# Batch 0's second pair of token tiles by seven products instead of eight, in a kernel whose order is planned

## The chip, the cores and the metric

The kernel runs on one core of a Trainium2 chip. The core has a matrix engine (TensorE, in the profile PE, with its weight loads shown apart as PEld), a vector engine (VectorE, DVE), a scalar engine (ScalarE, ACT), a general engine (GpSimd, POOL) and a queue engine (SyncE, SP). Each takes its instructions strictly in the order in which the program issued them, and waits at an instruction until what it needs is done. The metric is the device time of one execution in microseconds (us), as the median over several runs.

## The reference

Four batches of windowed attention with sink tokens, and a two-layer network with a squared ReLU over all 3072 tokens:

```python
B, H, S, D = 4, 8, 768, 64
keep = (pos[None, :] < 4) | ((rel >= 0) & (rel < 128))
a = softmax(where(keep, q @ k.T / sqrt(D), -1e9))
x = (a @ v).transpose(0, 2, 1, 3).reshape(B * S, H * D)     # 3072 x 512
g = maximum(x @ w_in, 0) ** 2                               # 3072 x 2048
out = g @ w_out                                             # 3072 x 512, float32
```

## The kernel before, in words

**Stages.** Each batch has 768 tokens, six tiles of 128, taken as three pairs of tiles (`s` in the attention, `u` in the second layer). For each batch q and k are transposed, scores are made (`ps`, L749), exponentials taken on ACT (`expm`, L769), masked on DVE (L778, L781) or POOL (L360), multiplied with the values (`po`, L817), normalised on DVE into `xn` (L834), and turned into `xT` (L866 on TensorE in batches 0 and 1, by DMA in 2 and 3). The first layer (`pm`, L895) writes PSUM tiles of 1024 columns; ReLU and square (L906, L908, L915, L917) leave `gT`, in two buffers: columns 0 to 511 (pairs 0 and 1) and 512 to 767 (pair 2). Batch 1's squares into the first buffer wait for the second layer of batch 0's pairs 0 and 1, by a dependency in `square`.

**The second layer has two forms.** `layer2` is the plain one: for each of the two tiles of a pair, 16 matmuls of 512 columns (L936), issued in eight parts of four matmuls, and one copy per tile into `osb` (L334). With `by_part` the two tiles take turns, so that a part needs only a quarter of `w_out` and of the squares. `layer2_fast` is an algebra of the Strassen kind: tiles a and b of the pair and the two halves of the 2048 inner columns make a 2 by 2 block matrix, and the two halves of the output columns another for `w_out`. Seven products of half size, each of eight matmuls of 256 columns (L1047), take the place of eight. It needs four block sums of `gT` on DVE (s1 to s4, L1005, 128 x 1024; s3 is written over tile b's lower half in `gT`, the others into four `sg` buffers), and four differences of blocks of `w_out` (wt1 to wt4, L977), which are made once by `weight_sums`. Its outputs share terms: two quarters are copied out early (`taken`, into `osb` and `u`), and pair sums (L1072), a last quarter (L1088) and the middle two quarters (L1095) are added on DVE before one store on SP (L1120).

In the kernel before, batch 0's pairs 0 and 1 go by `layer2`, its pair 2 and all pairs of batches 1 to 3 by `layer2_fast`. The last line of the call that decides it is `if b == 0 and u < 2` (L1189).

**What sets the order.** No loop of the program is the order of issue. Each step is an `op` with a key (its wanted place), engines with an assumed length on each, and the steps and buffers that it needs. `Plan.run` is a list scheduler: at every turn it takes the ready step with the earliest planned start (plus a lag), the key breaking ties, puts it on the engine where it would end first, and issues its instructions. `LATENCY` is the assumed time from one engine's end to another's start. `PLACES` shifts and stretches the keys of a group of steps and adds a lag; `NUDGES` does so for single steps by their number. Where an engine can be chosen (masks on POOL or DVE, copies on ACT or DVE), the plan chooses it. `warm` adds dummy matmuls (L327) in planned gaps before `WARM_UNTIL`. So the tables decide the order on each engine; on the chip semaphores hold it right whatever the lengths are. The order of the loads in each DMA queue is fixed by `dma_op`, but on POOL the loads stand in one line with its masks and copies.

PSUM has two pools, `att` and `den`, of two tiles each; a pair of the second layer holds one `den` tile from its first matmul to its last output step. There are two `osb` and two `u` buffers.

Of the kernel before, what the change touches and what calls it, by code (L numbers as in the profile page):

```python
# [16 lines left out]
LATENCY = 0.135  # L17
# [5 lines left out]
    ('att', 0, 0): (3.3, 1.08, 0.18), ('att', 0, 1): (3.285, 0.47, 0.38), ('att', 0, 2): (-0.2, 1.41, -0.24),  # L23
    ('att', 1, 0): (-1.415, 2.2, -0.42), ('att', 1, 1): (-0.385, 1.02, -0.22), ('att', 1, 2): (6.08, 1.06, 0.36),
    ('att', 2, 0): (-0.225, 0.25, -0.64), ('att', 2, 1): (-1.615, 1.17, -0.58), ('att', 2, 2): (0, 1.02, -0.06),
    ('att', 3, 0): (-0.075, 1.08, 0.1), ('att', 3, 1): (-0.04, 1.04, 0.04), ('att', 3, 2): (1.235, 0.72, 0.98),
    ('ev', 0, 2): (-0.16, 1.15, 0.78), ('ev', 1, 0): (0.585, 0.56, -0.48), ('ev', 1, 1): (0.47, 1.11, 0.24),
    ('ev', 1, 2): (-0.095, 1.18, 0.08), ('ev', 2, 0): (-0.22, 0.93, 0.28), ('ev', 2, 1): (0.015, 1.02, -0.46),
    ('ev', 2, 2): (1.345, 0.4, 1.32), ('ev', 3, 1): (-0.155, 1, 0.08), ('ev', 3, 2): (-0.055, 1.28, -0.44),
    ('l1', 0, 0): (-0.035, 1.27, 0), ('l1', 0, 1): (0.18, 0.85, 0.08), ('l1', 0, 2): (-0.6, 1.31, -0.4),  # L30
    ('l1', 1, 0): (4.96, 0.3, 0.74), ('l1', 1, 2): (0.265, 1.41, -0.28), ('l1', 2, 0): (-0, 0.59, 0.5),
    ('l1', 2, 2): (0.1, 1.22, -0.12), ('l1', 3, 0): (0.075, 0.91, 0.48), ('l2', 0, 0): (0.055, 0.81, 0.38),
    ('l2', 0, 1): (0.435, 1.16, 0), ('l2', 0, 2): (0.16, 1.12, -0.1), ('l2', 1, 0): (1.05, 0.56, -0.96),
    ('l2', 1, 1): (-0.425, 1.06, -0.1), ('l2', 1, 2): (-0.18, 1.03, 0.2), ('l2', 2, 0): (-0.115, 0.96, 0.58),
    ('l2', 2, 1): (2.185, 1.21, 1.32), ('l2', 2, 2): (2.75, 1, 0.74), ('l2', 3, 0): (-0.765, 0.25, 2.4),
    ('l2', 3, 1): (0.08, 0.81, 0.18), ('l2', 3, 2): (0.23, 1.94, 2.82), ('prep', 0, 0): (2.165, 1.2, -0.5),
    ('prep', 0, 1): (0.115, 1.01, -0.24), ('prep', 1, 0): (0.05, 0.87, 0.08), ('prep', 1, 1): (0.84, 1.23, 0.54),
    ('prep', 2, 0): (-0.005, 0.96, 0.24), ('prep', 3, 0): (-0.045, 1.08, 1.16),
    ('sink', 0, 0): (0.015, 1.11, -0.04), ('sink', 0, 1): (0, 1.12, -0.06), ('sink', 1, 0): (-0.225, 1.01, -0.06),
    ('sink', 3, 0): (-0.565, 0.62, 0.5), ('sum', 0, 2): (-0.14, 0.68, -0.34), ('sum', 1, 0): (-1.615, 0.44, -1.74),  # L40
    ('sum', 1, 1): (0.645, 0.91, -1.4), ('sum', 1, 2): (0.34, 1.45, 0.14), ('sum', 2, 0): (-0.655, 1.85, 0.06),
    ('sum', 2, 1): (-0.24, 1, 0.18), ('sum', 2, 2): (0.405, 1.27, 0.3), ('sum', 3, 0): (0.25, 2.36, 0.94),
    ('sum', 3, 2): (0.185, 1.17, 1.74), ('turn', 0, 0): (-0.56, 2.1, -0.62), ('turn', 0, 1): (0.11, 0.94, -0.14),
    ('turn', 0, 2): (-0.205, 1.01, 0.02), ('turn', 1, 0): (-0.2, 0.94, -0.02),
    ('turn', 1, 1): (-0.345, 1.33, -0.42), ('turn', 1, 2): (1.765, 2.5, -2.14), ('turn', 2, 0): (0, 1.05, 0),
    ('turn', 2, 1): (-0.26, 1.09, -0.3), ('turn', 3, 0): (-0.06, 1.05, -0.44), ('turn', 3, 1): (0.075, 0.56, 0.64),
    ('turn', 3, 2): (0, 1, 0.14), ('val', 0, 0): (0.345, 0.45, -0.28), ('val', 0, 1): (0.69, 0.58, -0.46),
    ('val', 0, 2): (-0.09, 0.78, -0.08), ('val', 1, 0): (-2.595, 0.7, 0.22), ('val', 1, 1): (0.035, 1.14, 0.06),
    ('val', 1, 2): (-0.65, 0.98, 0.64), ('val', 2, 0): (-1.11, 0.59, -1.94), ('val', 2, 1): (0.755, 0.42, -0.3),
    ('val', 2, 2): (-0.425, 1.6, -0.06), ('val', 3, 0): (0.1, 1.17, 0.6), ('val', 3, 1): (0.805, 0.25, 0.74),  # L50
    ('val', 3, 2): (0.105, 0.92, 2.28), ('wt', 0): (-0.205, 0.82, -0.32),
}
NUDGES = {
    4: (-0.022, 0.56), 16: (0, 0.14), 17: (-0.211, -0.38), 18: (0.48, -1.62), 19: (0, 0.4), 20: (0.364, -0.58),
    21: (0.004, 0.16), 22: (0.02, 0), 23: (0.016, 0.18), 24: (-0.06, -0.78), 25: (0.35, 1.84), 26: (-0.106, 0.66),
    27: (0.014, -0.64), 29: (-0.004, 0.86), 30: (0, 0.42), 31: (0.013, 0), 33: (-0.009, 0), 34: (-0.094, 0.5),
    36: (-0.027, 0.16), 37: (0.188, 0.08), 38: (-0.052, 0), 39: (-0.269, -0.82), 40: (-0.004, 0),
    41: (-0.419, 0.34), 42: (0.398, -2.86), 43: (0.134, -0.1), 44: (0.027, 0.14), 45: (0.009, 0), 46: (0.123, 0.66),
    47: (0.073, 0.9), 49: (0, 0.1), 51: (-0.102, -0), 52: (-0.278, -0.06), 53: (-0.001, 0.18), 56: (0.05, 0.1),
    57: (0.049, -0.16), 58: (0.016, -0.78), 60: (-0.008, -0.14), 61: (-0.013, 0), 62: (0, 0.22), 63: (-0.292, -0.2),  # L60
    64: (-0.079, 0.34), 65: (0.028, 0.64), 66: (-0.114, -0.38), 67: (0.099, -0.02), 68: (0.076, -0.28),
    69: (-0.851, 0.68), 71: (0.036, 0.22), 72: (-0.036, -0.24), 73: (0.024, 0.18), 74: (0.02, 0), 75: (-0.063, 0),
    76: (0, -0.04), 78: (0.042, 0.28), 80: (0.009, 0.26), 81: (0.023, 1.36), 82: (-0.02, 0.04), 83: (-0.008, -0.54),
    84: (-0.128, -0.42), 85: (-0.161, -0.36), 86: (0.003, 0), 87: (-0.004, 0.08), 88: (-0.069, 0),
    89: (-0.003, -0.16), 90: (-0.088, 0.02), 91: (0.016, -0.28), 92: (0.109, 0), 93: (0.015, 0.38),
    94: (0.043, -0.24), 95: (0.159, 0.04), 96: (-0.083, 0.04), 97: (-0.05, -0.3), 98: (-0.346, 0.8),
    99: (-0.435, 0.54), 100: (-0.21, -0.52), 101: (0.407, 1.44), 102: (0.013, 0.78), 103: (0.147, -0.08),
    104: (-0.112, -0.16), 105: (-0.121, -0.1), 107: (0.009, 0), 108: (0.214, 0.04), 109: (0.006, 0.08),
    111: (0.033, 0.86), 112: (0.046, 0.56), 113: (0.043, 0.6), 114: (-0.154, 0.42), 115: (-0.084, -0.16),
    116: (-0.145, -0.28), 117: (-0.026, -1.22), 118: (0.126, -0.62), 119: (-0.123, -0.24), 120: (0.115, 0.56),  # L70
    121: (0, -0.14), 122: (-0.121, 0.08), 123: (0, -0.2), 124: (0.034, -0.16), 125: (-0.168, 0.24),
    126: (0.017, -0.44), 127: (0.071, -0.82), 128: (-0.128, 0.1), 129: (-0.006, -0.08), 130: (0, -0.56),
    131: (0.402, 0.04), 132: (-0.056, 0), 133: (0.291, -0.28), 134: (-0.028, 0), 135: (0.064, -1.52),
    136: (-0.069, 0), 137: (-0.061, 0.54), 139: (-0.041, 0.32), 140: (-0.043, 0), 142: (-0.077, -0.12),
    143: (-0.069, 0.14), 144: (0.271, 0.26), 145: (0.008, 0.02), 146: (0.046, -0.52), 147: (0.008, -0.22),
    148: (0.006, 0.26), 149: (-0.028, 0.28), 150: (0.065, 0.06), 151: (0.051, 0.04), 152: (0.164, -0.12),
    153: (-0.401, 0.06), 154: (0.019, 0), 155: (-0.388, -0.64), 156: (-0.112, 1.16), 157: (0.287, 0.94),
    158: (-0.278, 1.3), 159: (-0.002, -0.18), 160: (0.118, 0.3), 162: (0.145, 0.5), 164: (0.158, 0.46),
    165: (0.095, 0), 166: (0.015, 0.02), 167: (0.055, 0), 168: (0.161, -0.48), 169: (-0.217, 0.24),
    171: (0.132, 0.52), 172: (0.011, -0.1), 173: (-0.036, 0.78), 174: (-0.047, -0.16), 175: (0.115, 0),  # L80
    176: (-0.342, 0.18), 177: (0, -0.02), 178: (-0.092, 0.58), 179: (0.041, 0.04), 180: (0.136, 0),
    186: (0.353, 0.28), 187: (-0.073, -0.02), 188: (-0.044, 0.48), 189: (-0.009, 0.06), 190: (0.057, -0.6),
    191: (-0.512, 1.18), 192: (0.405, 0.62), 193: (-0.012, -0.02), 194: (-0.003, 0.04), 195: (0.216, 0.94),
    196: (-0.08, -0.04), 197: (-0.038, 0.14), 198: (0.002, -0.54), 199: (0.12, 0.14), 200: (-0.304, 0),
    201: (-0.106, -0.12), 202: (0.038, 0.08), 203: (-0.001, -0.3), 205: (0.013, -0.44), 206: (-0.01, 0.46),
    207: (-0.003, 0.02), 208: (0.277, 0.98), 209: (0.006, -1.42), 210: (0.099, 0.36), 211: (0.041, 0),
    212: (0.006, 0), 214: (0.108, 0.54), 215: (0.057, 0.38), 216: (0.2, 0.22), 217: (-0.118, -0.12),
    218: (-0.002, 0.26), 219: (0.129, -0.22), 220: (0.008, -0.44), 221: (0.213, 1.02), 222: (0.464, -0.34),
    223: (-0.206, 0.1), 224: (0.064, 0), 225: (0.277, 0.32), 226: (-0.123, 0.62), 227: (0.015, 1.76),
# [170 lines left out]
def kernel(  # L260
# [22 lines left out]
    NKB = DM // 128  # L283
# [33 lines left out]
    op = P.op  # L317
# [566 lines left out]
    def layer1(b, key, fbs, c0, cw, need):  # L884
        P.group = ("l1", b, c0 // 256)
        n = len(fbs)
# [344 lines left out]
```

## Time and profile before

| | us |
|---|---|
| median of 10 runs (215.3 to 216.84) | 216.25 |
| the profiled execution: its own time | 216.69 |
| its span, first to last instruction | 214.9 |
| TensorE busy | 207.2 |
| DVE busy | 147.6 |
| ACT busy | 119.0 |
| POOL busy | 78.2 |
| first layer's matmuls (L895), busy | 87.4 |

A busy matmul is not a matmul's share of the stream: matmuls overlap, and a group's mean (309 ns for L895, 380 ns for L936, 273 ns for L1047) holds the time from its start to its modelled end. The distance from one start to the next is read from pieces of the chain of waits or from the list of instructions in order of time. The mean granted TensorE clock was 0.996.

### The profile page before, as it was taken

To read this page: it belongs to the slowest core of one execution; us is meant where nothing else is said; L and a number is where in the kernel's file an instruction comes from. 1 tells how busy PE (TensorE), PEld (TensorE's weight loads), DVE (VectorE), ACT (ScalarE), POOL (GpSimd) and SP (SyncE) were. 2 spreads that over 40 slices of the span, in tenths; PEclk is the share of its full clock that TensorE was granted. 3 is DMA by queue.
4 is the path that set the end of the run, shared out by engine and by line. 5 is a ranking of instruction groups with operands and counts; after the bars stand their busy time and mean duration, and the time that the engine had idled before them with its cause. 6 is when DMAs were issued, how large, how long until landed. Compare 5 with 4: busy or idle time off the path is not lost.

```text
span 214.9 us, 5183 instructions
## 1 busy us (share of the span) xinstructions
PE 207.2 (96%) x2189; PEld 160.3 (75%) x2189; DVE 147.6 (69%) x282; ACT 119.0 (55%) x149; POOL 78.2 (36%) x112
## 2 busy tenths in 40 slices
PE   7798999999999999999999999999999999999992
PEld 7468996589487645678897955876988955798892
DVE  5687658577958784677778757648886643466852
ACT  3697357455764669977654279769207046671110
POOL 7979474499969830884800000000001100000000
PEclk9999999999999999999999999999999999999998
DMA  5999999999999999999999543000325160000222
GB/s 152 287 172 203 174 199 215 159 128 205 156 137 145 197 217 124 157 122 157 117 220 111 149 104 93 3 0 0 52 98 95 54 149 0 0 3 2 98 101 98
DMA packets 93351, 26.06 MB, mean 121 GB/s; under 512 B 86800, under 2 KB 91280, under 8 KB 93328
## 3 DMA queue, kind: packets, MB, share of 16 engines
q0 software_dynamic: 69248, 12.59, 81.5%
q1 hardware_dynamic: 23896, 13.07, 28.2%
q8 instruction: 17, 0.28, 0.6%
q10 hardware_dynamic: 184, 0.07, 0.1%
q14 instruction: 6, 0.05, 0.1%
HBM read 27.30 MB, written 6.29 MB: 156 GB/s over the span
## 4 chain that ended last, share of the span: by engine, by line
PE 88%; DMA 6%; ACT 2%; DVE 1%; POOL 1%; SPq 0%; issue 0%
PE pm L895 38%; PE py L1047 28%; PE py L936 7%; PE po L817 6%; PE ps L749 5%; DMA w_in_sb<-in_moe_w_in_dram 4%; DMA qr<-in_k_dram 2%; PE pt L642 2%; ACT expm L769 1%; PE ya L1047 1%; PE px L866 1%; DVE xT L336 1%; POOL expm L360 1%; PE pk L708 1%; SPq L491 0%; ACT qs L334 0%
## 5 line engine op out<-in xcount | busy, mean ns | idle before, releaser
L895 PE MATMUL pm<-xT,w_in_sb 128*128 128x256 bf16 (+1 forms) x576 | 87.4, 309 | 0.8 <-DMA w_in_sb<-in_moe_w_in_dram 0.6
L895 PEld LDWEIGHTS <-w_in_sb 128*128 128x128 bf16 x576 | 62.4, 114 | 20.7 <-issue 1.3
L906 ACT ACTIVATE r<-pm 128x1024 bf16<-128x1024 f32 x42 | 43.1, 1025 | 33.0 <-PE pm L895 30.8
L769 ACT ACTIVATE expm<-ps 128x1024 bf16<-128x1024 f32 (+1 forms) x48 | 43.4, 951 | 15.5 <-PE ps L749 15.5
L917 DVE TENSOR_TENSOR gT<-r 128x1024 bf16<-128x1024 bf16 x35 | 24.2, 691 | 22.8 <-ACT r L906 22.6
L1047 PEld LDWEIGHTS <-gT 128*128 128x128 bf16 x336 | 31.1, 98 | 4.5 <-issue 1.2
L360 POOL TENSOR_SCALAR_AFFINE_SELECT expm<-expm 128x512 bf16<-128x512 bf16 x12 | 7.3, 632 | 73.3 <-ACT expm L769 68.7
L1047 PEld LDWEIGHTS <-sg 128*128 128x128 bf16 x240 | 22.9, 98 | 3.0 <-issue 0.5
L781 DVE TENSOR_TENSOR expm<-expm,tri 128x1024 bf16<-128x1024 bf16 x26 | 18.3, 706 | 7.7 <-ACT expm L769 7.5
L1047 PE MATMUL py<-wt,gT 128*128 128x256 bf16 x160 | 20.8, 273 | 0.0
L1047 PE MATMUL py<-wt,sg 128*128 128x256 bf16 x160 | 20.8, 273 | 0.0
L1047 PE MATMUL py<-w_out_sb,gT 128*128 128x256 bf16 x144 | 18.7, 273 | 0.0
L834 DVE TENSOR_TENSOR xn_sb<-po,rc 128x512 bf16<-128x512 f32 (+1 forms) x28 | 17.2, 615 | 1.0
L817 PE MATMUL po<-v,expm 128*128 128x65 bf16 x352 | 17.5, 193 | 0.4 <-DMA v<-in_v_dram 0.2
L817 PEld LDWEIGHTS <-expm 128*128 128x128 bf16 x352 | 16.4, 97 | 1.9 <-issue 0.4
L334 ACT ACTIVATE osb<-py 128x256 f32<-128x256 f32 (+1 forms) x15 | 6.6, 441 | 16.8 <-PE py L1047 11.7
L936 PE MATMUL py<-w_out_sb,gT 128*128 128x512 bf16 x64 | 15.7, 380 | 0.0
L749 PE MATMUL ps<-qkT 64*128 64x128 bf16 (+1 forms) x256 | 14.6, 238 | 0.0
L749 PEld LDWEIGHTS <-qkT 64*128 64x128 bf16 x256 | 8.0, 94 | 8.1 <-issue 7.5
L915 ACT ACTIVATE gT<-r 128x1024 bf16<-128x1024 bf16 x13 | 13.7, 1056 | 0.3
L817 PE MATMUL po<-vs,es 128*128 128x65 bf16 x128 | 13.0, 193 | 0.0
L817 PEld LDWEIGHTS <-es 128*128 128x128 bf16 x128 | 11.7, 97 | 0.3 <-issue 0.3
(78 smaller groups left out, 240.4 us busy)
## 6 DMA issues: line engine op xcount, KB each, us to landing
out_dram<-osb SPq DMA_DIRECT2D x11, 512.0 KB, 3.9
v<-in_v_dram POOLq DMA_DIRECT2D x24, 128.0 KB, 6.1
qn<-in_k_dram POOLq DMA_DIRECT2D x20, 128.0 KB, 8.6
qn<-in_q_dram POOLq DMA_DIRECT2D x20, 128.0 KB, 8.8
w_in_sb<-in_moe_w_in_dram POOLq DMA_DIRECT2D x4, 512.0 KB, 9.6
w_out_sb<-in_moe_w_out_dram POOLq DMA_DIRECT2D x4, 512.0 KB, 10.6
qr<-in_k_dram SPq DMA_DIRECT2D x4, 256.0 KB, 5.4
qr<-in_q_dram SPq DMA_DIRECT2D x4, 256.0 KB, 5.2
```

Source lines behind the costliest of these rows:

```text
L360: nc.gpsimd.affine_select(out=e_tile, in_=e_tile, compare_op=ALU.is_ge, fill=fill, base=i - 1, pattern=[[0, n], [1 if i else -1, 128]], ch ...
L749: nc.tensor.matmul(ps[:, h2, o:o + w], lhsT=qkT_sb[r, m, 1, c, :], rhs=qkT_sb[r, m, 0, qb:qb + w // 128, :], start=(i == 0 and not biased) ...
L769: nc.scalar.activation(out=x[:, :, o:512], in_=bank_t["s", b, s, m][:, :, o:512], func=AF.Exp, scale=scale)
L781: nc.vector.tensor_mul(y, y, tri.rearrange("p (o a) c -> p o (a c)", o=1).to_broadcast([128, 4, 256]))
L817: touch(("po", b, s, m0), e, nc.tensor.matmul(pv[:, i, h2, :], lhsT=lhsT, rhs=rhs, start=(n_ == 0), stop=(n_ == len(mms) - 1)), j)
L834: touch(("po", b, s, m0), e, nc.vector.tensor_tensor(out=xn_sb[:, 2 * s:2 * s + 2, 128 * (m0 + j0):128 * (m0 + j0 + nj)].rearrange("p i (j ...
L895: nc.tensor.matmul(pm[:, i, :], lhsT=w_in_sb[:, fb // 4, kb, fb % 4:512:4], rhs=xT[:, c0 // 256:(c0 + cw) // 256, kb, :], start=(kb == 0), ...
L906: nc.scalar.activation(out=o, in_=h, func=AF.Relu)
L915: nc.scalar.activation(out=g, in_=r, func=AF.Square)
L917: nc.vector.tensor_mul(g, r, r)
L936: touch((b, u), e, nc.tensor.matmul(pm[:, i, :], lhsT=gT_sb[t // 4][:, fb, 128 * (t % 4):128 * (t % 4) + 128], rhs=w_out_sb[:, fb, :], sta ...
L1047: ins = nc.tensor.matmul(y_, lhsT=x[:, i, :], rhs=r_, start=(first or tail and n == 2) and i == 0, stop=i == HB - 1, skip_group_check=not ...
```

## The change

Batch 0's pair 1 goes by `layer2_fast` instead of `layer2`. The planner's constants and all entries of both tables are new, so the order of issue is another one throughout:

```diff
-LATENCY = 0.135
+LATENCY = 0.261
 PLACES = {
-    ('att', 0, 0): (3.3, 1.08, 0.18), ('att', 0, 1): (3.285, 0.47, 0.38), ('att', 0, 2): (-0.2, 1.41, -0.24),
...
+    ('att', 0, 0): (-0.29, 1.39, -0.26), ('att', 0, 1): (1.755, 1.21, 0.6), ('att', 0, 2): (-1.795, 1.46, -0.16),
...
 NUDGES = {
-    4: (-0.022, 0.56), 16: (0, 0.14), 17: (-0.211, -0.38), 18: (0.48, -1.62), 19: (0, 0.4), 20: (0.364, -0.58),
...
+    4: (-0, -0.62), 16: (-0.025, -0.62), 17: (-0.253, 0.14), 18: (0.01, -0.32), 19: (0.316, 0.5),
...
-                            at(fm), {"pe": len(ms) * (0.7 if biased else 0.28) + (0.02 if b == 0 and not biased else 0.1)}, lambda e, f=scores, ms=ms: f(e, ms),
+                            at(fm), {"pe": len(ms) * (0.5 if biased else 0.23) + (0.02 if b == 0 and not biased else 0.1)}, lambda e, f=scores, ms=ms: f(e, ms),
...
-                        va = op(at(fm + 0.16), {"pe": (0.75 if s else 0.4) * len(js) / 2}, values,
+                        va = op(at(fm + 0.16), {"pe": (0.79 if s else 0.4) * len(js) / 2}, values,
...
-        a = op(key, {"pe": n * NKB * cw / 2350.0}, mm, takes=[bs],
+        a = op(key, {"pe": n * NKB * cw / 2372.0}, mm, takes=[bs],
...
-            a = op(keys(i, part), {"pe": 0.865}, mm, after=last + need + [w_out_op[part]],
+            a = op(keys(i, part), {"pe": 0.74}, mm, after=last + need + [w_out_op[part]],
...
         for u in range(NS):
-            if b == 0 and u < 2:
+            if b == 0 and u < 1:
                 layer2(b, u, lambda i, part, u=u: 0.408 + 0.466 * (4 * part + 2 * u + i) / 24, by_part=True)
             else:
                 layer2_fast(b, u, lambda n, u=u, b=b: b + 0.5 + 0.5 * (8 * u + 8 * n / 7.0) / 24)
```

The planned length of a `layer2_fast` product (0.88) and those of DVE, ACT and POOL steps stay as they were.

## The prediction

> **What bounds the kernel now.** I read the profile's first page (busy shares, slices), then who waited on TensorE, then the chain of waits in order of time, then engine busy time by stage, then the POOL queue in the first 25 us. From the first page:
>
> ```profile
> span 214.9 us, 5183 instructions
> PE 207.2 (96%) x2189; PEld 160.3 (75%) x2189; DVE 147.6 (69%) x282; ACT 119.0 (55%) x149; POOL 78.2 (36%) x112
> PE   7798999999999999999999999999999999999992
> ```
>
> TensorE (PE) is busy for 207.2 of 214.9 us and full from the fourth slice to the last. The missing 7.7 us are 1.5 before its first instruction, 3.9 after its last (211.0 to 214.9, the tail of the output) and about 2.3 between. All its own waits, by what ended them:
>
> ```profile
> PE pt L327 <- POOL ident L384: 1.5, 1, 1.5
> PE pt L642 <- DVE qs L336: 0.8, 1, 0.8
> PE pm L895 <- DMA w_in_sb<-in_moe_w_in_dram: 0.6, 2, 0.4
> PE pt L327 <- ACT expm L769: 0.2, 1, 0.2
> PE po L817 <- DMA v<-in_v_dram: 0.2, 1, 0.2
> PE pm L895 <- DVE xT L336: 0.2, 1, 0.2
> ```
>
> Only the last lies after 25 us (74.5). So from 23.1 to 211.0 an instruction taken off TensorE moves the end by its own length, and one on another engine costs nothing until TensorE waits for it. The chain of waits gives lengths; its columns are start, length, work:
>
> ```profile
> 12.93 1.17 POOL expm L360 x2
> 14.09 8.98 DMA w_in_sb<-in_moe_w_in_dram
> ...
> 54.16 1.73 PE py L936 x8
> ...
> 56.59 1.83 PE py L936 x8
> ...
> 66.39 0.86 PE py L936 x4
> ...
> 68.70 0.86 PE py L936 x4
> ...
> 70.29 1.73 PE py L936 x8
> ...
> 151.70 6.11 PE py L1047 x56
> ```
>
> The five L936 pieces, 32 matmuls, are pair 1 of batch 0. The last line is 56 matmuls of 256 columns in a row, as many as seven products have, without a gap. Stages around the change (columns: length, then busy us of PE, PEld, DVE, ACT, POOL):
>
> ```profile
> 45.00:55.00 10.00, 10.00 (x101) 8.98 (x99) 8.30 (x13) 5.99 (x9) 10.00 (x12) 1.00 2.06 174
> 55.00:65.00 10.00, 10.00 (x99) 6.64 (x98) 7.39 (x14) 5.86 (x9) 7.99 (x11) 1.00 2.31 144
> 65.00:75.00 10.00, 9.81 (x154) 7.11 (x149) 8.29 (x20) 5.62 (x9) 9.16 (x12) 1.00 2.59 173
> ```
>
> VectorE (DVE) is next: 23.98 of 30 us busy there, 6.02 idle. The clock column is 1.00.
>
> **The change, part by part.**
>
> *TensorE work removed and added.* Removed: 7.01 us by the five pieces (1.73 + 1.83 + 0.86 + 0.86 + 1.73), or 6.92 at the plain spacing of 1.73 / 8 = 0.216 us. The difference is what the pieces' borders hold. Added: 56 matmuls of 256 columns, 6.11 us by the last row. Saved: 0.81 to 0.90; I take 0.85. It is on the path whole, because TensorE has no slack there. TensorE also loads 56 stationary blocks instead of 32; a load takes 98 ns in the L936 and L1047 groups and a 256-column matmul follows the other by 6.11 / 56 = 0.109 us, so a load stays just hidden.
>
> A rule speaks against this. The row: 0.216 us per 512-column matmul, 0.109 per 256. The Trainium skill, "TensorE: Matmul & The Clock Gate", section "Back-to-back issue gap", gives a sustained spacing of about 81 ns at 128 columns and 131 ns at 512, and says that N/2.4 + 2.5 ns is for isolated matmuls only. On a straight line between its two figures 256 columns take an estimated 98 ns: 32 x 131 ns = 4.2 us out and 56 x 98 ns = 5.5 us in, so the change would cost 1.3 us and end near 217.6. Its formula gives 215.8 and 109.2 ns and a gain of 0.79 us. The trace agrees with the formula in a full stream, and the sum goes by the trace.
>
> *VectorE work added.* Four sums of 691 ns (the group "sg<-gT"): 2.76 us. Output: two copies of 0.60 on ScalarE (ACT) go; in come three copies of a quarter (0.38 on ACT, 0.42 on DVE), two pair sums and a last-quarter sum (0.42 each) and a middle sum of 0.69. With copies on ACT, ACT pays 1.14 - 1.20, so nothing, and DVE 2.76 + 1.95 = 4.71 us, against 6.02 idle in 45 to 75: it fits, 1.3 us left. I price it at 0; the cover is that idle time, and the rows of the same work at 56.3 to 59 in pair 2 delay no product. Without cover: the four weight differences (1.22 each) end at 50.8, and in 45 to 55 only 1.70 us are idle, so sums placed there overshoot by 2.76 - 1.70 = 1.06; the far end is all 2.76. Below nothing there is no gain from added work.
>
> *Waits inside the products.* The product of s2 waits for the copy of the first result, the product with the fourth weight difference for a pair sum and the copy into u. Each has at least one product (0.87) between it and what it waits for, against copies of 0.38 to 0.43; no L1047 matmul shows in the list of waits. Cost 0; were a product to follow its copy directly, 0.4 to 0.5 each, at most two. Behind a waiting product the whole in-order TensorE queue stands, scores of batch 1 first, whose exponentials ACT then gets late.
>
> *Later begin, buffers, stores.* The old pair could start with a quarter of the weights; the new needs all 16 blocks of its squared activations (the last two squares run on ACT at 35.9 and 39.1, 1.05 each, so ready by 40.2) and the weight differences (44.0 to 50.8). The old one began at 54.0, so nothing is late: 0, and up to 1.7 (two old parts that served as filler at 54) if its sums miss that time. Its place can lie later: then batch 1's squares for the first 512 columns, due from about 77, wait for it; the old pair ended at 72.0. Pairs 1 and 2 together need six sum buffers of four; one wait of at most a product, 0.87, on DVE, with masks behind it; I take 0, since three pairs in a row at 192 to 211 run without a gap. The store (issued at 72.7 on SP, 0.33) stays one; behind it in SP's queue are transposes of batch 2 from 73.1. A store later by a us delays them by a us, and the first score that reads them is over 20 us off: 0.
>
> *The new order.* The constants make no instruction. Semaphore latency 0.135 to 0.261, scores, biased scores and layer-1 lengths move toward the trace (non-biased score pair planned 0.66, now 0.56; trace 0.55). A layer-2 part goes 0.865 to 0.74 where four matmuls last 0.86, and values go 0.75 to 0.79 where 24 last 0.73: eight remaining parts planned 1.0 us short. What that does is not in this trace, so bounds. After 23 us: TensorE idles about 0.4 us up to 211; gain at most 0.4. Loss: its nearest waits elsewhere are 0.2 to 0.8 each; I take 0, the row nearest (188 us with 0.4 idle and DVE and ACT gaps everywhere). Before 23 us: gain at most 2.2, which is 1.1 idle in 7 to 23 (14.89 of 16 busy) and 19 dummy warm-up matmuls at 0.06 us. Loss: the POOL queue, which issues the loads of the first layer's weights:
>
> ```profile
> 10.25 0.80 POOL L448 DMA_DIRECT2D w_in_sb<-in_moe_w_in_dram  x1
> 11.11 0.54 POOL L360 TENSOR_SCALAR_AFFINE_SELECT tri<-tri 128x128 bf16<-128x128 bf16 x2
> 12.93 1.22 POOL L360 TENSOR_SCALAR_AFFINE_SELECT expm<-expm 128x512 bf16<-128x512 bf16 x2 [1.27 <-ACT expm L769]
> 14.09 1.51 POOL L448 DMA_DIRECT2D w_in_sb<-in_moe_w_in_dram  x2
> ```
>
> Loads three and four wait behind a mask: 1.27 for ACT and 1.22 of work. One more mask put ahead costs 2.49; one less frees as much. Of the two I take 0, the row as it stands.
>
> *Sum.* The profiled execution took 216.69 (span 214.9, 1.79 around it), 0.44 above the median of 216.25. 216.69 - 0.85 = 215.84 in its terms; 215.4 against the median.
>
> **The rivals.**
>
> *A, slower: a second mask ahead of the weight loads on POOL.* For it: every early key is changed, the mask may go to POOL or DVE, and TensorE's layer 1 at 20.5 and 23.1 already waited for these loads. Against: TensorE waited only 0.6 us in all, and other work can move up. Price 2.49 - 0.85 = +1.64: 217.9. It decides from a delay of 0.85 us that TensorE cannot fill.
>
> *B, faster: the front is repacked.* The mask leaves POOL, loads three and four go at 11.7 instead of 14.1, and filler replaces dummies. For it: 2.2 us of idle and dummies. Against: the q and k loads and their casts pace this stretch (0.8 us wait on qs). Price -0.85 - 2.2 at most: 213.2; half of it, 214.3.
>
> *C, no change: VectorE takes it back.* Sums fall between weight differences and the key copies of batch 1 and overshoot by 1.06: 216.25 - 0.85 + 1.06 = 216.5. For it: 8.30 of 10 busy in 45 to 55. Against: 6 us idle over the longer stretch.
>
> *D, the change does not do what it says:* 56 short matmuls last as long as 32 long ones or longer. The rows of 0.216 and 0.109 us exclude it, and it gets no chance.
>
> **How the numbers follow.** A measurement can tell about 0.3%, 0.65 us. Forecast 0.42, its own range 215.0 to 215.9 (0.45 gained on the idle, or one wait of 0.5): 0.30 of it below 215.6, 0.12 within. B 0.20, faster. C 0.12: half same, half slower. A 0.26, slower. So faster 0.50, same 0.18, slower 0.32. The range leaves out the extreme ends of A and B, a tenth each: 213.5 to 218.0.
>
> **What would show it.** Right: L936 with 32 matmuls and L1047 with 56 more, the sum of both 0.8 to 0.9 less; ten seven-product pairs become eleven, DVE busy 4 to 6 us longer; no new TensorE wait over 0.2 us after 25 us; the third weight load issued at 14 us; last matmul near 210.1. Wrong: a TensorE wait on sg, u or qkT between 50 and 75 (C); the weight loads' issue moved by over 1 us, with a wait of pm on them (A, or B if earlier); a wait in batches 1 to 3 that I give no cause for, where an order fixed in advance met an engine later than planned.

## The result and the profile after

The changed kernel takes 217.24 us (median of 14 runs, 215.86 to 218.1), the kernel before 216.12 (51 runs): ratio 1.0053, 95% interval 1.0038 to 1.0067. It is 0.5% slower, where 0.4% faster was forecast. Its runs spread over 2.2 us, those of the kernel before over 1.6. Three executions of it were profiled, of 216.12, 216.63 and 217.78 us (spans 214.3, 214.9 and 216.0). The first is near the low end of the runs (215.86 to 218.1) and shows almost nothing wrong. From its first page:

```profile
span 214.3 us, 5270 instructions
PE 206.3 (96%) x2218; PEld 162.8 (76%) x2218; DVE 147.4 (69%) x279; ACT 121.1 (56%) x154; POOL 85.8 (40%) x122
PE   5899999999999999999999999999999999999992
```

The first digits are lower than before (58 for 77), the rest is full. What TensorE itself waited for, in that execution:

```profile
PE pt L327 <- POOL ident L384: 2.5, 1, 2.5
PE pt L642 <- DVE qs L336: 0.6, 1, 0.6
PE ps L749 <- ACT es L716: 0.3, 1, 0.3
PE pm L895 <- DMA w_in_sb<-in_moe_w_in_dram: 0.2, 1, 0.2
```

And in the third, which is 1.7 us longer:

```profile
PE pt L327 <- POOL ident L384: 2.5, 1, 2.5
PE pm L895 <- DMA w_in_sb<-in_moe_w_in_dram: 1.7, 2, 1.1
PE ps L749 <- ACT es L716: 0.3, 1, 0.3
PE po L817 <- DVE expm L781: 0.2, 1, 0.2
```

What differs most between these two executions of the same kernel is the wait of the first layer (`pm`) for its weights (`w_in`): 0.2 us in one, 1.7 in the other. The chain of waits of the first execution (start, length, work) leads from the weights back through POOL's line of work without a gap to the first step on it, the triangles for the masks (`tri`):

```profile
1.70 0.10 POOL tri L360
...
12.21 10.73 DMA w_in_sb<-in_moe_w_in_dram
...
22.98 7.18 PE pm L895 x64
...
45.32 0.87 PE py L1047 x8
...
46.87 2.62 PE py L1047 x24
...
50.16 0.87 PE py L1047 x8
...
53.90 1.75 PE py L1047 x16
...
209.43 0.91 PE ya L1047 x16
```

Pair 1's seven products are the four pieces from 45.32 on, 6.11 us in sum, as the forecast had them. POOL's own list, in order of time (start, length, instruction, and in brackets the idle time before it):

```profile
1.70 0.54 POOL L360 TENSOR_SCALAR_AFFINE_SELECT tri<-tri 128x128 bf16<-128x128 bf16 x2 [1.17 <-DVE head_rows L369]
2.20 0.29 POOL L384 TENSOR_SCALAR_AFFINE_SELECT ident<-ident 128x128 bf16<-128x128 bf16 x1
...
6.68 1.96 POOL L521 DMA_DIRECT2D v<-in_v_dram  x2
8.62 0.92 POOL L448 DMA_DIRECT2D w_in_sb<-in_moe_w_in_dram  x1
9.53 1.95 POOL L521 DMA_DIRECT2D v<-in_v_dram  x2
11.46 2.24 POOL L448 DMA_DIRECT2D w_in_sb<-in_moe_w_in_dram  x3
```

The same list of the kernel before has:

```profile
1.15 0.29 POOL L384 TENSOR_SCALAR_AFFINE_SELECT ident<-ident 128x128 bf16<-128x128 bf16 x1 [0.63 <-DVE ident L366]
...
5.83 1.96 POOL L521 DMA_DIRECT2D v<-in_v_dram  x2
```

Before, the triangles stood behind the second weight load, at 11.11. Now they come first, wait until VectorE has filled their tile, and push `ident` (the unit matrix that TensorE's first matmuls read) from 1.15 to 2.20 and the first load from 5.83 to 6.68. The three later weight loads, on the other hand, are issued back to back ahead of the mask, from 11.46 on, where before two of them waited until 14.09.

To divide the time, I take two instants from the lists of TensorE's instructions and the chain: the start of the first layer's third unit (the stretch of 64 matmuls) and the end of the last `ya` piece, the last products of the last pair. In the first profile of before they are:

```profile
23.12 7.18 PE pm L895 x64
...
210.07 0.91 PE ya L1047 x16
```

| execution | profiled, us | third unit starts | wait of pm for w_in | from there to the end |
|---|---|---|---|---|
| before, first and second profile | 216.69, 216.47 | 23.12, 22.92 | 0.6, none | 187.86, 187.83 |
| after, first | 216.12 | 22.98 | 0.2 | 187.36 |
| after, second | 216.63 | 23.18 | none | 187.67 |
| after, third | 217.78 | 24.31 | 1.7 | 187.70 |

So the changed kernel is two things: a front that ends at scattered times, up to 1.4 us later than before, and a rest that is only 0.15 to 0.5 us shorter, not 0.85.

### The profile page after: what moved, and what is told of

Its sections match the earlier page's. It is cut to its first block, busy times and chain, and to the rows that moved or that the text cites. A ratio compares the mean times of both kernels' runs of the same rounds, so it can differ in the third digit from the quotient of the medians.

```text
span 214.3 us, 5270 instructions
## 1 busy us (share of the span) xinstructions
PE 206.3 (96%) x2218; PEld 162.8 (76%) x2218; DVE 147.4 (69%) x279; ACT 121.1 (56%) x154; POOL 85.8 (40%) x122
## 4 chain that ended last, share of the span: by engine, by line
PE 87%; DMA 5%; POOL 5%; issue 1%; ACT 1%; POOLq 0%; ACTq 0%
PE pm L895 38%; PE py L1047 31%; PE po L817 6%; DMA w_in_sb<-in_moe_w_in_dram 5%; PE ps L749 5%; PE py L936 3%; POOL v L521 2%; PE pt L642 2%; PE ya L1047 1%; POOL w_in_sb L448 1%; POOL vs L690 1%; PE px L866 1%; PE pk L708 1%; ACT r L906 0%; POOL sg L360 0%
## 5 line engine op out<-in xcount | busy, mean ns | idle before, releaser
L906 ACT ACTIVATE r<-pm 128x1024 bf16<-128x1024 f32 x44 | 45.1, 1024 | 36.1 <-PE pm L895 34.7
L917 DVE TENSOR_TENSOR gT<-r 128x1024 bf16<-128x1024 bf16 x38 | 26.7, 704 | 29.9 <-ACT r L906 29.8
L1047 PEld LDWEIGHTS <-gT 128*128 128x128 bf16 x368 | 34.0, 98 | 4.4 <-issue 0.9
L1047 PEld LDWEIGHTS <-sg 128*128 128x128 bf16 x264 | 25.1, 98 | 3.4 <-issue 0.6
L360 POOL TENSOR_SCALAR_AFFINE_SELECT expm<-expm 128x512 bf16<-128x512 bf16 x18 | 13.1, 750 | 27.4 <-DVE osb L1072 14.2
L1047 PE MATMUL py<-wt,sg 128*128 128x256 bf16 x176 | 22.9, 273 | 0.0
L1047 PE MATMUL py<-wt,gT 128*128 128x256 bf16 x176 | 22.7, 273 | 0.0
L1047 PE MATMUL py<-w_out_sb,gT 128*128 128x256 bf16 x160 | 20.8, 273 | 0.0
L817 PE MATMUL po<-vs,es 128*128 128x65 bf16 x128 | 12.9, 193 | 0.0
L1047 PE MATMUL py<-w_out_sb,sg 128*128 128x256 bf16 x88 | 11.4, 273 | 0.0
L521 POOL DMA_DIRECT2D v<-in_v_dram x12 | 10.9, 916 | 0.6 <-DMA w_in_sb<-in_moe_w_in_dram 0.4
```

Source lines behind the costliest of these rows:

```text
L360: nc.gpsimd.affine_select(out=e_tile, in_=e_tile, compare_op=ALU.is_ge, fill=fill, base=i - 1, pattern=[[0, n], [1 if i else -1, 128]], ch ...
L521: return [nc.gpsimd.dma_start(out=v_sb[b % 2][:, t, :, 0:D], in_=v[b, :, 128 * t:128 * t + 128, :].rearrange("h p d -> p h d"))]
L817: touch(("po", b, s, m0), e, nc.tensor.matmul(pv[:, i, h2, :], lhsT=lhsT, rhs=rhs, start=(n_ == 0), stop=(n_ == len(mms) - 1)), j)
L906: nc.scalar.activation(out=o, in_=h, func=AF.Relu)
L917: nc.vector.tensor_mul(g, r, r)
L1047: ins = nc.tensor.matmul(y_, lhsT=x[:, i, :], rhs=r_, start=(first or tail and n == 2) and i == 0, stop=i == HB - 1, skip_group_check=not ...
```

## The experiments

The first three repeat the two kernels. From the fourth on the steps are issued from a written-out list (step, engine, PSUM pool) that was read out of the planner's run of either kernel, so that parts of the two orders can be joined or one step moved with all else left in place.

**1 to 3. The two kernels again**, the changed one twice, the kernel before once, without an edit. They were to show what varies.

> The changed kernel once more, as it is, for another execution's profile. Its profiled execution of 216.12 us lies at the low end of its 14 runs (215.86 to 218.1, median 217.24), and in it TensorE waits 0.3 us after 25 us. Theory 1 (a transfer or an engine that is just in time: late in some executions, early in others): a slower execution shows, at one place, a TensorE wait that the first profile lacks, 0.5 to 2 us long, and the rest of the chain unchanged. Theory 2 (the start: loads land at other times and the whole chain begins later): the first layer's long stretch of 64 matmuls begins later than 22.98 us by what the execution is longer. Theory 3 (TensorE's own matmuls last longer, clock or spacing): no new wait, the clock under 1.00 or the plain spacing of 0.109 us larger.

> The kernel before once more, for a second profile beside the first (216.69 us, upper end of its runs of 215.3 to 216.88). Theory 1 expects the same list of waits within 0.3 us and nothing new in the middle. Theory 2 expects the begin of the 64 matmuls to move with the time (23.12 us in the first). Theory 3 expects a change of the spacing.

> The changed kernel a third time. As for the first repeat: where the execution is slower than 216.12 us, theory 1 expects the same new wait as there, theory 2 a later begin of the 64 matmuls, theory 3 a larger spacing.

Measured: the first two rows and the last two of the table above. The start theory held: 1.1 us of the 1.2 us between the second and the third execution of the changed kernel lie before the third unit (23.18 to 24.31), and the rest is the same to 0.03. (Between the first and the second it is 0.2 of 0.5; the other 0.3 lies in the rest, and run 10 comes back to it.) The clock was 0.996 to 1.0 in all, and the spacing of a 256-column matmul the same, so theory 3 fell. The waits in the middle are small and steady (0.3 on `es`), so theory 1 explains no scatter. With 6 to 8 executions each, the times themselves say little: 216.73 and 217.08 for the changed kernel, 216.63 for the one before, where the runs of before beside them had 215.87.

**4. Old front, changed rest.**

```diff
-order = changed
+order = before[: third unit of layer 1] + [sink step of batch 1] + changed[third unit of layer 1 :]
```

> The changed kernel with the order of the kernel before up to the first layer's third unit (the stretch of 64 matmuls at 23 us), on all engines; from there on the changed order as it is (both orders have issued the same steps by then, but for one sink step of batch 1, which stays where the change has it). Start theory (the first 23 us cost the time, by loads that land later or at scattered times): the loss goes, 215.6 to 216.1 us, no slower than before (ratio 0.997 to 1.001), and the 64 matmuls begin at 23.1 within 0.2. Rival, rest theory (the loss is in the order after 23 us): it stays, 216.9 to 217.3, ratio 1.004 to 1.006.

Measured: 215.78 us, ratio 0.9981 (0.9966 to 0.9997). The loss is gone; third unit at 23.04, 187.71 from there on.

**5. Changed front, old rest** (both plain pairs; the sink step of batch 1 again stands where the change has it).

```diff
-order = before
+order = changed[: third unit of layer 1] + before[third unit of layer 1 :]
```

> The reverse: the kernel before (both plain pairs) with the changed order up to the third unit of the first layer, and its own order from there on. Start theory: 217.0 to 217.6, ratio 1.004 to 1.007, and the 64 matmuls begin between 23.0 and 24.5, differing between executions. Rest theory: as before, 216.1, ratio 1.000.

Measured: 217.17 us, ratio 1.0059 (1.0033 to 1.0085): the front alone makes the whole loss, in a kernel without the new products. Its profiled execution is one of the longest of its twelve (218.45 us). From its list of TensorE's waits and its chain:

```profile
PE pm L895 <- DMA w_in_sb<-in_moe_w_in_dram: 2.1, 2, 1.3
```

```profile
12.20 12.41 DMA w_in_sb<-in_moe_w_in_dram
...
24.66 7.18 PE pm L895 x64
```

The load that ends the wait was issued 1.9 us earlier than the one in the kernel before (14.09) and landed 1.5 us later: it took 12.41 us instead of 8.98. (In the changed kernel's first and third execution the same load took 10.73 and 12.38.) From the third unit to the end it needs 187.86 us, exactly the figure of the kernel before.

**6. Changed order, pair 1 by eight parts.**

```diff
-[sums s1 s3 s2 s4] ... p5 p7 p1 p6 p3 p4 p2 [x, u, pair sums, middle, first quarter]
+part(0,0) part(1,0) part(0,1) part(1,1) part(0,2) part(1,2) part(0,3) part(1,3) [two copies]
```

> The changed order kept step for step, but pair 1 of batch 0 by eight parts of four 512-column matmuls: a part in the place of each product, the eighth directly behind the seventh, the four sums and the output additions on VectorE left out, two copies put in. If the seven products save their 0.73 to 0.85 us of TensorE time in this order, it is that much slower than the changed kernel: 217.8 to 218.1, ratio to before 1.008. If the sums on VectorE take the saving back, it is equal to the changed kernel, 217.1 (1.005), or faster.

Measured: 216.92 us, ratio 1.0047 (1.0027 to 1.0068), beside 1.0053 for the changed kernel. By time alone the seven products save nothing that can be told in this order. The profile separates it from the front: 188.15 us from the third unit to the end, against 187.36 to 187.70 with the products. So the saving is 0.45 and 0.48 in two executions and 0.79 in one; and against the 187.85 of the kernel before, with the same amount of work, the new order after the front is 0.3 us worse.

**7. Old order, the later plain pair by seven.**

```diff
-            if b == 0 and u < 2:
+            if b == 0 and u == 1:
...
-part part ... part part | ps | part part ... (pair 0, 54 to 72 us)
+p5   p7   ... p1   p6   | ps | p3   p4   p2     sums at 51 to 53 and 63 us on VectorE
```

Two further steps of VectorE go to ScalarE.

> The order of the kernel before kept, and of batch 0's two plain pairs the one that runs later (pair 0, at 54 to 72 us) by seven products, each in the place of a part, the eighth place left empty; its sums on VectorE where that sits idle (51 to 53 and 63 us), and two steps of VectorE moved to ScalarE. Algebra theory (0.85 us less on TensorE moves the end by as much): 215.2 to 215.5, ratio 0.996 to 0.997. VectorE theory (VectorE is full from 65 to 75 us, 8.29 of 10, and its added output steps of 1.5 us hold the steps that open batch 1's first layer at 74.5): TensorE waits 0.5 to 1 us there, 215.9 to 216.3.

Measured: 216.48 us, ratio 1.0024 (1.0008 to 1.0040): slower, and 188.58 us from the third unit to the end, 0.7 more than before. TensorE's list at 70 us, and ScalarE's:

```profile
70.08 0.40 PE L866 MATMUL px<-ident,xn_sb 128*128 128x128 bf16 x4 [0.16 <-DVE xn_sb L834]
70.92 0.40 PE L866 MATMUL px<-ident,xn_sb 128*128 128x128 bf16 x4 [0.44 <-DVE xn_sb L834]
```

```profile
71.49 0.38 ACT L334 ACTIVATE osb<-py 128x256 f32<-128x256 f32 x1 [5.22 <-DVE osb L1095]
```

VectorE is full there, and the pair's output sums stand ahead of the normalisations that batch 1's transposes wait for: the VectorE theory, with a larger loss than it had. Part of it is this experiment's own: the copy of the first output quarter was put on ScalarE behind the middle sum, and ScalarE idled 5.22 us at its head with other copies queued behind. It shows that the saving can be lost on VectorE, not that it must be.

**8 and 9. The triangles alone.** In the changed kernel they go back, in the kernel before they go to the front:

```diff
 POOL, changed kernel
-tri ident bias head_rows vs v v w_in v v w_in w_in w_in qn
+ident bias head_rows vs v v w_in v v w_in w_in tri w_in qn
```

```diff
 POOL, kernel before
-ident bias head_rows vs v v w_in v v w_in tri mask w_in w_in qn
+tri ident bias head_rows vs v v w_in v v w_in mask w_in w_in qn
```

> The changed kernel with one step moved on one queue: the two triangle selects on POOL (0.54 us), which the change issues ahead of all of POOL's other work and so makes them wait for VectorE's fill, go behind the fourth load of the first layer's weights; all else as changed. Triangle theory (POOL's loads begin 0.7 us later in the changed order, 6.5 to 6.8 instead of 5.8 to 6.0 us, and all weights land later by that or more): loads begin by 6.0 and most of the front's 1.2 us goes, 216.0 to 216.4, ratio 0.999 to 1.002. Rival, grouping theory (three weight loads back to back, ahead of the mask, disturb each other and the loads of v): the loss stays, 216.9 to 217.3, ratio 1.004 to 1.006.

> The kernel before with the same step alone moved the other way: the two triangle selects ahead of POOL's other work, where the change has them. Triangle theory: the whole of POOL's line begins 0.7 to 0.9 us later and the kernel loses 0.7 to 1.2 us, 216.8 to 217.2, ratio 1.003 to 1.006. Grouping theory: same as before, 1.000.

(The expectation put them behind the fourth weight load; the list that ran has them behind the third.) Measured: the changed kernel with the triangles moved back 216.21 us, ratio 1.0008 (0.9986 to 1.0030); the kernel before with them in front 216.93, ratio 1.0044 (1.0026 to 1.0062). One step of 0.54 us, moved on one queue, is worth 0.45% in either kernel. The grouping of the weight loads is not the cause: the first of the two keeps it almost as changed and loses nothing clear of noise, the second has the old grouping and loses. POOL's list in the first:

```profile
1.15 0.29 POOL L384 TENSOR_SCALAR_AFFINE_SELECT ident<-ident 128x128 bf16<-128x128 bf16 x1 [0.63 <-DVE ident L366]
...
5.60 1.96 POOL L521 DMA_DIRECT2D v<-in_v_dram  x2
```

The loads begin at 5.60, and `pm` waits for no weight at all; its third unit starts at 22.18. In the second kernel they begin at 6.93:

```profile
6.93 1.96 POOL L521 DMA_DIRECT2D v<-in_v_dram  x2
```

and the third unit starts at 23.39, where the two profiles of before have 23.12 and 22.92. What the two runs don't separate by time: the step holds `ident` too, and with it TensorE's first instruction (2.55 instead of 1.50). In the second kernel's profile TensorE still waits 0.5 us for the weights at 20 and 23 us, so in that execution their landing and not TensorE's own late begin sets the third unit.

**10. Old front, changed rest, and two sums moved.**

```diff
 VectorE
-s1 s3 s2 s4 mask mask norm norm    wt1 wt3 wt2    wt4
+s1 s3       mask mask norm norm s2 wt1 wt3 wt2 s4 wt4
```

> The kernel with the old front and the changed rest (0.9981 of before), and on VectorE two of pair 1's four sums moved: s2 and s4 not ahead of the masks of batch 0's last pair, but behind their normalisation and between the weight differences. Sums theory (sums that run beside POOL's masks last 1.0 to 2.1 us instead of 0.69, and the masks behind them hold the values at 40 us): TensorE's wait of 0.2 and the gap of 0.55 at 40 us go, 0.3 us less, 215.4 to 215.6, ratio 0.996 to 0.997. Rival: TensorE waits later for s2, s4 or a weight difference instead (45 to 54 us): 215.8, 0.998.

Measured: 215.56 us, ratio 0.9984 (0.9965 to 1.0004), against 215.78 and 0.9981 without the move: by time not to be told apart. By the profile 187.36 us (22.32 to 209.68) from the third unit to the end instead of 187.71, and the wait of `po` on a mask is gone. VectorE's list without the move, and POOL's masks beside it (run 4):

```profile
35.41 1.00 DVE L1005 TENSOR_TENSOR gT<-gT 128x1024 bf16<-128x1024 bf16 x1
36.34 1.11 DVE L1005 TENSOR_TENSOR sg<-sg,gT 128x1024 bf16<-128x1024 bf16 x1
37.49 2.06 DVE L1005 TENSOR_TENSOR sg<-gT,sg 128x1024 bf16<-128x1024 bf16 x1
39.47 1.28 DVE L781 TENSOR_TENSOR expm<-expm,tri 128x1024 bf16<-128x1024 bf16 x2
```

```profile
35.24 1.67 POOL L360 TENSOR_SCALAR_AFFINE_SELECT expm<-expm 128x512 bf16<-128x512 bf16 x2 [0.74 <-issue]
...
37.76 1.23 POOL L360 TENSOR_SCALAR_AFFINE_SELECT expm<-expm 128x512 bf16<-128x512 bf16 x2
```

VectorE's with the move:

```profile
42.52 0.68 DVE L1005 TENSOR_TENSOR sg<-sg,gT 128x1024 bf16<-128x1024 bf16 x1
...
46.52 0.68 DVE L1005 TENSOR_TENSOR sg<-gT,sg 128x1024 bf16<-128x1024 bf16 x1
```

The same sum takes 2.06 us in one place and 0.68 in the other. In the changed kernel's first execution the delay fell elsewhere, on POOL's masks and on VectorE's own two behind the sum:

```profile
37.42 1.00 DVE L1005 TENSOR_TENSOR sg<-gT,sg 128x1024 bf16<-128x1024 bf16 x1
38.35 2.15 DVE L781 TENSOR_TENSOR expm<-expm,tri 128x1024 bf16<-128x1024 bf16 x2
```

```profile
37.84 2.11 POOL L360 TENSOR_SCALAR_AFFINE_SELECT expm<-expm 128x512 bf16<-128x512 bf16 x2
```

There VectorE's masks end 17.52 us after the third unit's start, against 17.71 in run 4, no `po` waits on a mask, and that is the execution with a rest of 187.36. In the other two the sum took 2.06 us and POOL's masks 1.23, as in run 4, with rests of 187.67 and 187.70.

**11. As run 10, and all first weight loads ahead of the sink values on POOL.**

```diff
 POOL
-... head_rows vs v v w_in v v w_in tri mask w_in w_in qn
+... head_rows v v w_in v v w_in w_in w_in tri vs mask qn
```

> As the run before, and on POOL all four weight loads of the first layer and batch 0's first v loads go ahead of the sink values (1.97 us), which are not needed before 18 us, and ahead of the triangles and the mask. If the front is set by when POOL begins its loads: they begin at 4 instead of 5.9 us, the weights land 1 to 2 us earlier, 214.2 to 215.0, ratio 0.992 to 0.995. If it is set by the DMA engines' rate (about 200 GB/s from 1 us on, whoever asks first): the loads of q and k land later by what the others land earlier, and it ends within 0.3 of the run before, or slower, as the attention's begin waits.

Measured: 215.50 us, ratio 0.9980 (0.9965 to 0.9995). The loads begin 2.4 us earlier than in run 10 and nothing is won: third unit at 22.47 instead of 22.32, no wait for weights in either. From its POOL list and TensorE's waits:

```profile
3.68 1.94 POOL L521 DMA_DIRECT2D v<-in_v_dram  x2
```

```profile
PE pt L642 <- ACT qs L334: 0.8, 1, 0.8
```

The wait is for ScalarE's cast of a load of q, and that load came later than in run 10. ScalarE's list there and here:

```profile
10.59 0.63 ACT L334 ACTIVATE qs<-qr 128x512 bf16<-128x512 f32 x1
```

```profile
11.26 0.63 ACT L334 ACTIVATE qs<-qr 128x512 bf16<-128x512 f32 x1 [0.90 <-DMA qr<-in_q_dram]
```

A late begin of POOL's loads costs, an earlier one is worth nothing. That fits the second case of the expectation, in which the loads share one rate and q pays for what the weights gain; with one profile of each, it is not more than a fit.

**12. As run 10, pair 1 by eight parts** (the edit of run 6 in the order of run 10).

> The run with the old front and the two sums moved (0.9984 of before, third unit of the first layer to last matmul 187.1 us in its profile), but pair 1 of batch 0 by eight parts, each in the place of a product and the eighth behind the seventh, without the sums and the output additions. Algebra theory (with the sums out of the masks' way the seven products save what TensorE's lengths say, 0.73 to 0.85 us): the stretch from the third unit to the last matmul is 187.8 to 188.0, the time 0.7 to 0.9 us more than that run, 216.3 to 216.5, ratio 1.001 to 1.003. Rival (the saving is lost on VectorE also there): 187.1 to 187.4 and 215.6 to 215.8, ratio 0.998 to 0.999.

Measured: 215.89 us, ratio 1.0012 (0.9990 to 1.0033), against 0.9984 with the products. The two pieces of its chain:

```profile
22.57 7.18 PE pm L895 x64
...
209.82 0.91 PE ya L1047 x16
```

From the third unit to the end 188.16 us, against 187.36 with the products: 0.80. (These figures run to the end of the last matmul, the expectation's 187.1 to its start.) With the sums out of the way the algebra saves, by the profiles, what TensorE's lengths say; by time the difference, 0.28%, is no larger than the uncertainty of the two ratios.

The versions of runs 4 and 11 are faster than the kernel before by intervals that barely exclude 1 (upper ends 0.9997 and 0.9995); that of run 10 reaches 1.0004.

## Why the prediction was wrong, point by point

*TensorE work removed and added (0.85).* Right. The added products took 6.11 us, and run 12 against run 10 gives 0.80 where nothing hides it. The row decided rightly against the sustained figures of the Trainium skill ("TensorE: Matmul & The Clock Gate", section "Back-to-back issue gap"): by the estimate from those the change would cost 1.3 us, and it saves 0.8.

*Which pair the five pieces were.* Wrong reading. The planner's order, read out for the experiments, has pair 1 at 35.5 to 47.6 us and pair 0 in the five pieces from 54 on. I took the pair from its number. The sum was not touched (both pairs are 32 matmuls), but what I wrote of the old pair's begin, its filler at 54 and its end at 72.0 was about the wrong pair. In the changed kernel the plain pair is early too, and the seven products follow at 45.32. (A second slip of reading: the list of TensorE's waits had a seventh line, `po` on `xT`, 0.2 us at 93, so two waits and not one lay after 25 us. No term rests on it.)

*VectorE work added (0, at most 1.06, far end 2.76).* The mechanism of rival C was real, its place and reason were not mine. The sums stand at 35 to 39 us, not at 45 to 55, and there they ran beside POOL masks and lasted up to 2.06 us; TensorE's values behind them waited 0.2 for a mask. Run 10 takes it away: 0.35 us. In 65 to 75 us VectorE's busy time rose from 8.29 to 8.95 and nothing broke. That window of the first profile after (length, busy us of PE, PEld, DVE, ACT, POOL):

```profile
65.00:75.00 10.00, 9.66 (x144) 7.91 (x141) 8.95 (x18) 7.28 (x12) 8.76 (x13) 1.00 2.95 124
```

*Waits inside the products (0), later begin, buffers and stores (0).* Right: no L1047 matmul waited in any of the changed kernel's profiles, and TensorE's lists name no wait on a store or a buffer.

*The new order after 23 us (0).* Off by 0.3: 188.15 us with eight parts in the new order against 187.85 in the old (runs 6 and 12 against the two profiles of before). A new wait of 0.3 on `es` at 66 us is in runs 6 and 12 and not in before, but that it is the whole 0.3 was not tried.

*The new order before 23 us (0).* This is the step that failed. I bounded it by one mask more or less ahead of the weight loads and took the row as it stood. What moved was another step, and it moved further: the triangles, from behind the second weight load to the head of POOL's line. The fence that I showed for this bound has the line of the triangles in it, and the diff gives step 4 of the list, which they are, a lag of -0.62 where it had +0.56. The front then cost 0.59% (run 5); the triangles are worth 0.45% in either direction (runs 8 and 9). The remaining 0.1% lies within these intervals. Whether the late loads alone carry the loss, or the late `ident` too, is not shown.

*Rival A (217.9)* had the right queue, sign and effect, weight loads that land late and TensorE waiting for them at 20 and 23 us, but a wrong step: the third and fourth loads went ahead of the mask, not behind another. *Rival B's* event, loads three and four early, did happen (about 12.2 and 12.9 instead of 14.1 and 14.8), and gave nothing.

*The sum, with what the runs showed:* +1.2 for the front (run 5 against before), +0.3 for the new order after it, -0.80 for the algebra, +0.35 for the sums beside the masks make +1.05; measured +1.12. The close fit is partly luck: the same terms give +1.5 for run 6, where 0.9 was measured with an interval of 0.6 to 1.5. The range of 213.5 to 218.0 held the time; the side was wrong.

## What to carry to other kernels

Where a change replans an order, read the first few steps of each queue, and above all of the queue that issues loads, before costing anything else: here half a microsecond at its head outweighed 0.8 us of removed matmuls at the place of the change. One profile of a kernel whose runs scatter can be one of its luckiest; compare two or three, cut at a fixed instant, before asking where the time went. Joining the front of one order to the rest of the other, and then moving one step, settled in four runs what comparing two whole orders could not.

## What the runs showed of the hardware that was not expected

A sum of 128 x 1024 bf16 values from two SBUF tensors on VectorE takes 0.68 to 0.69 us alone, and 1.00, 1.11 and 2.06 us where POOL's selects on `expm` run at the same time (run 4 against run 10). Either side can be the longer one: 2.06 for the sum and 1.23 for the two selects in run 4, 1.00 and 2.11 in the changed kernel's first execution. The Trainium skill, "GPSIMD Engine Reference", section "Specifications", says that POOL's interfaces to SBUF are shared with VectorE and that VectorE instructions with two SBUF inputs contend; the runs agree.

A load's time to landing is not its own. The third weight load took 8.98 us when issued at 14.09 (first profile of before), and 10.73, 12.38 and 12.41 when issued at 11.9 to 12.2, directly behind the second (two executions of the changed kernel, and run 5). Asked for about 2 us earlier, it landed between 0.1 us earlier and 1.5 us later. Moving the triangles, and with them the begin of POOL's loads, from 5.6 - 6.0 to 6.5 - 6.9 us cost 0.8 to 1.0 us of the median time; a begin at 3.7 gained nothing. The begin alone does not give the landing: of the changed kernel's executions the one that began at 6.50 had its third load at 24.27, the one that began at 6.68 at 22.94. What in the transfers makes this scatter is left open.
